# Retuning the issue order of an attention and MLP kernel for a first load as traced and dummy products up to the first k^T v

## The chip, the cores and the metric

The kernel runs on one core of a Trainium2 chip. The metric is the device time of the whole program in microseconds (us), from repeated executions on the chip. "Before" is the kernel without the change and "after" the kernel with it. The engines are called PE (TensorE), PEld (TensorE's weight loads), ACT (ScalarE), DVE (VectorE), POOL (GpSimd) and SP (SyncE). A number such as L870 is a line of the kernel. The change adds eight lines high up, so L870 of before is L878 of after.

## The reference

Eight batches, eight heads, 576 rows (four tiles of 128 and a "tail" of 64), 64 columns per head. Linear attention without a softmax is followed by a normalisation and a residual MLP with a token mixing step.

```python
kv  = einsum('bhsd,bhse->bhde', k, v)                  # k^T v, per head 64 x 64
out = einsum('bhsd,bhde->bhse', q, kv)
x   = out / sqrt(mean(out*out, -1) + 1e-6) * g_norm    # then (b, 576, 512)
a1  = alpha1 * x + beta1
tok = einsum('ts,bsd->btd', w_tok, a1)                 # w_tok: 576 x 576
u   = x + lam * tok
ch  = maximum((alpha2 * u + beta2) @ w_ch1, 0) @ w_ch2 # 512 -> 2048 -> 512
y   = u + lam * ch
```

## The kernel before

The kernel is written as a pool of operations with priorities. When it is built, a small model inside the kernel plays all engines against each other, picks for each free engine the ready operation with the best priority, and so makes one list per engine. On the chip each engine works through its list in order. Semaphores make it wait where an operand is not there yet, and it doesn't look past the operation that waits. So the model's clock, its load times and the priorities decide the order, and the chip decides the time.

The parts that the change touches:

```python
        self.cold = 12.0          # until then a TensorE product is modelled at twice its cost
...
        clock = [3.4]             # when the first load begins to flow
...
        def pe_cost(o):
            if t < self.cold:
                return 2 * o.cost["PE"]
...
            # TensorE has nothing to do now: put a dummy product into its list
            if self.warm is not None and free["PE"] <= t + 1e-9 and t > 0.5:
                o = self.dummy(t, owner)
                if o is not None:
                    seq.append(o)
                    free["PE"] = o.start + (0.43 if t < self.cold else 0.217)
...
def group(o):
    return "%s %s %.2f" % (o.tag, "".join(e[0] for e in sorted(o.cost)), min(o.cost.values()))
ORDER = {                         # corrections to the priority of such a group
    'ch1.0 AD 0.62': 58.4,
    ...
    'wt P 0.03': -1.5,
    'x.01 DP 0.43': -6.1,
}
```

(The comments are mine; three dots are cuts.) The dummy products are there to keep TensorE's clock up while it has nothing to do. They become fixed members of TensorE's list.

The second load, of batch 1, has a modelled time of its own, which the change leaves alone. ScalarE (or VectorE) rounds the loaded q for TensorE:

```python
        def load_q(b, pri, halves=(None,)):
                ...
                    w=STK(i) if x is None else [("st", i, x)], dma_us=3.0 if x is None else 1.5,
                    pri=pri, kind="L")
...
        def round_q(b, pri, halves=((0, 8),)):
                        ...
                        s = st[:, i].rearrange("p (h c d) -> p c h d", h=NH, c=4)
                        return copy_to(e, m, qr[:, c:c + 2, h0:h1], s[:, c:c + 2, h0:h1])
                    ...
                    P.op({"DVE": dve_us(ne, 2), "ACT": act_us(ne)}, f, r=[("st", i, y) for y in hs],
                         w=[("qr", x, y) for x in (c, c + 1) for y in hs], pri=pri, port=True)
...
        round_in(1, -195)         # batch 1: its priority is far ahead of its need
```

Names used below. "Batch 1 k^T v" is L698 before and L706 after. "tok.00" and "tok.01" are the token mixing products of batch 0's two column halves (L998, L1006). "ub" is u in bf16, cast on ScalarE (L494, L502) and transposed on TensorE (L1126, L1134). "The first ch1 product" is the first of `a2 @ w_ch1` (L1167, L1175); from there on TensorE does little but MLP products.

## Time and profile before

| | before |
|---|---|
| time, median of 3 (range) | 352.69 us (352.56 to 352.96) |
| TensorE busy, of a span of 351.1 us | 344.6 us (98%) |
| TensorE's granted clock, 0 to 11 us, 11 to 16 us, after | 0.90, 0.53, 1.00 |
| first k^T v of batch 0 | 11.03 us |
| transposes of w_tok begin | 24.93 us |
| tok.00, batch 1 k^T v begin | 30.65, 34.19 us |
| first ch1 product | 40.78 us |
| from there to the end | 310.3 us |

The table is to be read as two parts, the first 41 us and the 310 us after them. The start of the first ch1 product tells how much an issue order wins or loses in the first part. The prediction below shows the lines.

### The profile page before, as it was taken

The numbers are of one execution on the slowest core, as the hardware profiler recorded it, in microseconds if no ns is written. First come the engines' busy times: TensorE is split into PE (matmuls) and PEld (weight loads), VectorE is DVE, ScalarE is ACT, GpSimd is POOL, SyncE is SP. The second block draws the span as 40 slices with busy tenths as digits, with TensorE's granted clock in tenths as the row PEclk, the third lists the DMA queues.
The fourth block names the chain that finished last, engine by engine and source line by source line (L and its number), as shares of the span: only waits on it lengthen the run. The fifth ranks groups of instructions, "written<-read, shape, count | busy, mean of one in ns | idle before, by whom it ended". The sixth has DMA issues, their size and how long they took to land.

```text
span 351.1 us, 5353 instructions
## 1 busy us (share of the span) xinstructions
PE 344.6 (98%) x2086; PEld 209.3 (60%) x2114; DVE 234.1 (67%) x408; ACT 144.0 (41%) x259; POOL 148.9 (42%) x145
## 2 busy tenths in 40 slices
PE   8899999999999999999999999999999999999996
PEld 3688864567765545647764545547764544457644
DVE  7457589865898786868867778868856683710043
ACT  2653774116823275226722275117731264016500
POOL 3877545027367493147332583148512562140000
PEclk9699999999999999999999999999999999999999
DMA  6899999979935899449952199329922210410022
GB/s 172 255 208 306 206 206 324 186 142 282 226 90 89 206 277 152 93 125 316 200 60 61 74 307 266 65 85 282 264 55 60 83 40 6 100 60 30 2 60 90
DMA packets 90949, 53.62 MB, mean 153 GB/s; under 512 B 56864, under 2 KB 86376, under 8 KB 90924
## 3 DMA queue, kind: packets, MB, share of 16 engines
q1 hardware_dynamic: 60176, 30.81, 36.9%
q0 software_dynamic: 30496, 22.29, 33.4%
q8 instruction: 16, 0.26, 0.3%
q10 hardware_dynamic: 252, 0.18, 0.2%
q14 instruction: 9, 0.07, 0.1%
HBM read 38.20 MB, written 9.44 MB: 136 GB/s over the span
## 4 chain that ended last, share of the span: by engine, by line
PE 96%; DMA 2%; SPq 1%; issue 0%; DVE 0%; ACT 0%
PE ps L1167 36%; PE ps L1195 36%; PE ps L1060 9%; PE ps L689 4%; PE ps L698 2%; DMA st<-in_v_dram 2%; PE ps L998 2%; PE ps L1295 1%; PE ps L1073 1%; PE ps L870 1%; PE ps L898 1%; PE ps L1352 1%; PE ps L967 1%; PE ps L703 1%; PE ps L945 1%
## 5 line engine op out<-in xcount | busy, mean ns | idle before, releaser
L1195 PE MATMUL ps<-w,ht 128*128 128x512 bf16 (+2 forms) x576 | 134.9, 376 | 0.8 <-issue 0.3
L1167 PE MATMUL ps<-a2t,w 128*128 128x320 bf16 (+1 forms) x760 | 133.8, 327 | 0.3
L1167 PEld LDWEIGHTS ps<-a2t,w 128*128 128x128 bf16 x768 | 73.4, 98 | 44.8 <-DVE ht L1153 0.3
L1152 ACT ACTIVATE ht<-ps 128x640 bf16<-128x640 f32 (+1 forms) x106 | 69.0, 653 | 56.6 <-PE ps L1167 55.5
L1195 PEld LDWEIGHTS ps<-w,ht 128*128 128x128 bf16 x592 | 55.9, 98 | 59.6 <-issue 0.8
L1213 POOL TENSOR_TENSOR xm<-xm,lc 128x512 f32<-128x512 f32 x28 | 36.6, 1308 | 95.0 <-DVE lc L1203 94.6
L820 POOL TENSOR_TENSOR xm<-yn,g_bc 128x512 f32<-128x512 f32 x28 | 39.5, 1411 | 47.9 <-DVE yn L815 44.8
L1203 DVE TENSOR_TENSOR lc<-ps,lam_bc 128x512 f32<-128x512 f32 (+2 forms) x37 | 25.0, 675 | 48.8 <-PE ps L1195 44.4
L802 ACT ACTIVATE sq<-ps 128x512 f32<-128x512 f32 (+1 forms) x35 | 20.7, 593 | 36.2 <-PE ps L689 35.9
L689 PE MATMUL ps<-kvc,qt 128*128 128x128 f32 x112 | 32.5, 381 | 0.0
L1065 DVE TENSOR_TENSOR xm<-ps,xm 128x512 f32<-128x512 f32 x28 | 19.0, 689 | 18.3 <-PE ps L1060 17.9
L1060 PE MATMUL ps<-rt,wt 128*128 128x512 bf16 x109 | 30.4, 383 | 0.1
L698 PE MATMUL ps<-vr,kr 128*128 128x128 f32 x112 | 30.3, 386 | 0.0
L804 DVE TENSOR_REDUCE small<-sq 128x8 f32<-128x512 f32 (+1 forms) x35 | 23.6, 676 | 8.4 <-ACT sq L802 8.2
L817 DVE TENSOR_TENSOR rt<-yn,ge 128x512 bf16<-128x512 f32 x27 | 24.4, 912 | 0.4
L815 DVE TENSOR_TENSOR yn<-ps,small 128x512 f32<-128x512 f32 (+1 forms) x35 | 23.9, 689 | 0.8
L689 PEld LDWEIGHTS ps<-kvc,qt 128*128 128x128 f32 x112 | 22.1, 199 | 2.3
L1153 DVE TENSOR_SCALAR ht<-ps 128x512 bf16<-128x512 f32 (+1 forms) x22 | 16.1, 736 | 10.3 <-PE ps L1167 10.2
L698 PEld LDWEIGHTS ps<-vr,kr 128*128 128x128 f32 x112 | 21.6, 200 | 0.8 <-DMA vr<-in_v_dram 0.3
L494 ACT ACTIVATE ub<-xm 128x512 bf16<-128x512 f32 (+1 forms) x17 | 9.3, 563 | 22.5 <-DVE xm L1065 22.4
L1060 PEld LDWEIGHTS ps<-rt,wt 128*128 128x128 bf16 x112 | 10.9, 97 | 11.7
L681 DVE TENSOR_TENSOR st<-st 128x1024 bf16<-128x1024 f32 x12 | 16.2, 1367 | 0.2 <-ACT st L494 0.2
(152 smaller groups left out, 366.1 us busy)
## 6 DMA issues: line engine op xcount, KB each, us to landing
out_dram<-xm SPq DMA_DIRECT2D x31, 256.0 KB, 2.6
kr<-in_k_dram POOLq DMA_DIRECT2D x7, 1024.0 KB, 8.9
vr<-in_v_dram POOLq DMA_DIRECT2D x7, 1024.0 KB, 12.6
st<-in_q_dram SPq DMA_DIRECT2D x7, 1024.0 KB, 9.5
w<-in_moe_w_ch_dram POOLq DMA_DIRECT2D x8, 512.0 KB, 17.5
st<-in_k_dram SPq DMA_DIRECT2D x2, 512.0 KB, 7.2
st<-in_v_dram SPq DMA_DIRECT2D x2, 512.0 KB, 7.7
st<-in_q_dram SPq DMA_DIRECT2D x2, 512.0 KB, 8.7
```

Source lines behind the costliest of these rows:

```text
L689: P.op(F, lambda e, _: e.matmul(t.flat()[:, 128 * pr:128 * pr + 128], a(), m(), start=True, stop=True), r=r, w=[t], kind="F", **kw)
L698: P.op(cost, lambda e, _, h=h, c=c: e.matmul(t.flat()[:, 128 * (h - h0):128 * (h - h0) + 128], flat(kr[:, s, h, c:c + 2, :]), flat(vr[:, s ...
L804: P.op({"DVE": dve_us(512)}, lambda e, _: e.tensor_reduce(out=small[rows, s4], in_=sq[rows, s2], axis=AX.X, op=ALU.add), r=[("sq", s2)], w ...
L815: P.op({"DVE": dve_us(512)}, lambda e, _: e.tensor_tensor(out=hview(yn[rows, s3, :]), in0=hview(t.flat(rows)), in1=bc, op=ALU.mult), r=[t, ...
L817: P.op({"DVE": dve_us(512), "POOL": pool_us(512)}, lambda e, _: e.tensor_tensor(out=rto, in0=yn[rows, s3, :], in1=ge1[rows, :], op=ALU.mul ...
L820: P.op({"POOL": pool_us(512)}, lambda e, _: e.tensor_tensor(out=hview(x), in0=hview(yn[rows, s3, :]), in1=g_bc[rows, None, :].to_broadcast ...
L1060: P.op({"PE": 0.216}, lambda e, _, sc=sc: e.matmul(t.flat(), wt[:, sc, 128 * c:128 * c + 128], rt[:, sc, :] if sc < 4 else rtt[:], start=( ...
L1152: return e.activation(dst, src(), ACT.Relu)
L1167: return e.matmul(o, w1[:, dj, 128 * fj:128 * fj + 128], m, start=(dj == 0), stop=(dj == 3))
L1195: P.op({"PE": 0.004 + n * 0.212 / 512}, lambda e, _: e.matmul(t.flat()[:, 0:n], ht[:, fj, 128 * c:128 * c + 128], w2[:, fj, lo:hi], start= ...
L1203: o = P.op({"DVE": dve_us(n)}, lambda e, _: e.tensor_tensor(out=lc[:, lo:hi], in0=t.flat()[:, 0:n], in1=lam_bc[:, lo:hi], op=ALU.mult), r= ...
L1213: lambda e, _: e.tensor_tensor(out=x, in0=x, in1=lc[:, lo:hi], op=ALU.add),
```

## The change

No operation of the kernel is added or removed. Its own model is corrected with numbers from a trace: the first loads, and the time from which TensorE runs at full clock (5.4 us instead of 12.0). The model now asks for dummies at half their former modelled length between 5.4 and 12 us, so more of them, up to the first k^T v. A new set of priorities was then tuned on that model. The intent is a first stretch in which the model's times are the chip's.

```diff
-        self.cold = 12.0
+        self.cold = 5.4
@@
-        clock = [3.4]
+        clock = [2.6]
@@ ORDER = {
-    'sums.01 P 0.11': 52.5,
-    'tok.01 P 0.12': -17.8,
-    'w1.3 P 0.93': -5.8,
-    'wt P 0.03': -1.5,
+    'qtr.01 AD 0.40': -90.0,
+    'sums.00 A 0.30': -85.1,
+    'sums.01 P 0.11': 37.6,
+    'w2.3 P 0.93': 49.5,
+    'wt P 0.03': -48.7,
     ...                       (21 entries before, 29 after; six keys are in both)
@@ def load(b, pri):             first load, b == 0
-                        w=[f + "ft"], dma_us=1.0, pri=pri, kind="L")
+                        w=[f + "ft"], dma_us=0.8, pri=pri, kind="L")
-                            w=["qft"], dma_us=1.0, pri=pri, kind="L")
+                            w=["qft"], dma_us=0.9, pri=pri, kind="L")
-                        w=[("st", i, x)], dma_us=1.5, pri=pri, kind="L")
+                        w=[("st", i, x)], dma_us=1.9 if x == 0 and f != "v" else 1.35, pri=pri, kind="L")
```

More of the change, by code (lines that the diff above doesn't have):

```diff
@@ L453 @@
 ORDER = {
-    'ch1.0 AD 0.62': 58.4,
-    'ch2.1 S 0.45': -1.4,
-    'norm.1 D 0.69': 53.4,
-    'norm.1 P 0.07': 22.6,
-    'norm.2 D 0.69': -31.4,
-    'norm.5 D 0.69': -65.9,
-    'norm.5 P 1.33': -5.6,
-    'norm.6 DP 0.69': 56.8,
-    'norm.6 P 1.33': 57.3,
-    'qtr.1 P 0.07': -5.1,
-    'qtr.4 DP 0.69': -34.3,
-    'round_in.4 DP 1.23': -28.1,
-    'round_in.5 DP 1.23': -37.9,
-    'sums.01 P 0.11': 52.5,
-    'tok.01 P 0.12': -17.8,
-    'tok.4 D 0.69': 35.8,
-    'tok.5 P 0.22': -10.7,
-    'w1.0 P 0.93': 6.2,
-    'w1.3 P 0.93': -5.8,
-    'wt P 0.03': -1.5,
-    'x.01 DP 0.43': -6.1,
+    'ch1.0 AD 0.62': 60.6,
+    'ch2.3 D 0.69': 8.9,
+    'load.0 DP 0.15': 92.7,
+    'load.0 DP 0.25': 21.1,
+    'load.0 P 0.50': 71.9,
+    'load.1 P 0.93': -6.5,
+    'norm.1 DP 0.69': 64.1,
+    'norm.2 D 0.20': 39.9,
+    'norm.4 D 0.20': 26.5,
+    'norm.5 DP 0.69': 28.6,
+    'norm.5 P 1.33': 36.3,
+    'qtr.00 P 0.12': -31.1,
+    'qtr.01 AD 0.40': -90.0,
+    'qtr.4 DP 0.69': -34.3,
+    'qtr.4 S 2.40': -19.4,
+    'round.01 ADP 0.43': -10.0,
+    'round.t AD 0.45': -55.9,
+    'round_in.3 DP 1.23': 5.0,
+    'sums.00 A 0.30': -85.1,
+    'sums.01 P 0.11': 37.6,
+    'tok.1 P 0.22': 10.9,
+    'tok.5 P 0.22': -29.1,
+    'tok.5 P 0.75': 2.0,
+    'w2.3 P 0.93': 49.5,
+    'wt P 0.03': -48.7,
+    'x.00 D 0.69': -17.1,
+    'x.00 DP 0.69': -3.1,
+    'x.01 D 0.69': 13.5,
+    'x.01 P 1.33': 48.4,
 }
```

## The prediction

> **What bounds the kernel now.** I began with the page of the kernel before: the busy row of the engines, the slices, then the chain of work that ended last.
>
> ```profile
> PE 344.6 (98%) x2086; PEld 209.3 (60%) x2114; DVE 234.1 (67%) x408; ACT 144.0 (41%) x259; POOL 148.9 (42%) x145
> ...
> PEclk9699999999999999999999999999999999999999
> ...
> PE 96%; DMA 2%; SPq 1%; issue 0%; DVE 0%; ACT 0%
> ```
>
> TensorE is busy for 98% of the span and is 96% of the chain. The kernel therefore ends when TensorE has done its real work once at full clock, plus whatever TensorE wasted on the way. The waste is of three kinds: idle, half clock, and dummy products (which count as busy). The clock row shows the second slice alone, 8.8 to 17.6 us, below full. To size the waste I asked for stretches of the span; the columns are the stretch, its length, busy time and count of PE, PEld, DVE, ACT and POOL, granted clock, DMA share and GB/s.
>
> ```profile
> 0.00:11.00 11.00, 8.56 (x22) 2.84 (x22) 7.55 (x20) 3.85 (x7) 4.88 (x17) 0.90 0.71 204
> 11.00:16.00 5.00, 4.97 (x20) 4.44 (x20) 1.74 (x4) 2.96 (x7) 3.75 (x5) 0.53 0.96 289
> 16.00:25.00 9.00, 9.00 (x66) 7.50 (x66) 5.06 (x14) 5.27 (x13) 6.48 (x9) 1.00 0.87 155
> 25.00:41.00 16.00, 15.86 (x147) 13.17 (x148) 11.60 (x28) 7.19 (x14) 10.23 (x15) 1.00 1.36 274
> 41.00:60.00 19.00, 18.95 (x114) 11.79 (x115) 15.26 (x29) 12.90 (x26) 8.68 (x10) 1.00 1.35 258
> ...
> 320.00:351.00 31.00, 28.13 (x175) 16.82 (x174) 7.23 (x12) 7.74 (x11) 0.00 (x0) 1.00 0.13 43
> ```
>
> From 41 us on TensorE idles some 3.8 us of 310, and 2.9 of that is the last stretch, the final multiply, add and store. There is nothing for an issue order to win there beyond about 0.9 us. All else is in the first 41 us. The same stretches asked for the dummy product's line alone give 13 dummies in 16 to 25 us, 8 in 25 to 41 and 1 just after 11; none follows. The timeline of TensorE shows the start:
>
> ```profile
> 1.04 5.35 PE L1295 MATMUL ps<-hot 128*128 128x512 bf16 x14 [1.04 <-DVE hot L1262]
> 6.32 1.98 PE L1308 MATMUL ps<-xm,w 1*128 1x512 f32 x4
> 8.33 0.22 PE L1337 MATMUL ps<-ident,w 8*128 8x8 f32 x1
> 8.49 1.15 PE L1295 MATMUL ps<-hot 128*128 128x512 bf16 x3
> 11.03 0.80 PE L870 MATMUL ps<-vr,kr 128*128 128x256 f32 x2 [1.39 <-ACT vr L494]
> ```
>
> Line 870 is the first k^T v. It waits for the first half of v, which landed at 10.33 us (issued at 2.88, 7.45 under way in the chain), and for a rounding on ScalarE. The dummies stop at 9.64, so TensorE stands idle 1.39 us. Fine stretches place the clock: full at 8.8, half from about 8.85 to about 15.68.
>
> **What the Trainium skill says.** "TensorE: Matmul & The Clock Gate", section "What's actually happening": the array runs at half clock by default, and a free-running window of about 3.4 us with enough activity releases it. The trace agrees: dummies start 0.43 us apart from 1.04 to 5.28 us and 0.22 apart after (the granted clock reads 1.00 throughout, so the spacing is the better witness). 15.68 minus 8.85 is 6.83 us, two such windows. Section "Wait — 56ns, not 53.3ns?" gives 426.7 and 215.7 ns per 512-column product, as here. One thing is not explained by that page: the clock fell at 8.85, before the idle of 1.39 us began, after a window that was nearly all "busy", but 2 us of it with line 1308, fp32 products with one row of the array in use. I suspect that these count for little. "DMA: Bandwidth & Descriptors", section "Issuing engines are not separate DMA queues", says that the queues share the same 16 engines; the trace agrees, with DMA share above 1.3 from 25 to 60 us.
>
> **The change part by part.** No operation of the kernel is added or removed; the kernel holds a small model by which it lists its own instructions when built, and the edit changes that model. (1) The time until which a product costs double goes from 12.0 to 5.4 us. Dummies fill the modelled gaps, so their number follows from it. Before, they were laid at 0.43 us up to the first product: 17, plus two doubled 0.9 us for line 1308. Now, some 10 at 0.43, then (10.0 - 5.4 - 1.8)/0.217, about 13, so 23: 10 x 0.427 + 13 x 0.217 + 1.98 = 9.1 us from 1.04, ending near 10.3 instead of with a 1.39 us gap. The gap shrinks to about half a microsecond. (2) The first loads get the times traced: 2.6 + 0.8 + 2.0 = 5.4 for the first tail against 5.3 traced. The order of these loads does not change, so the first half of v still lands near 10.3 and the first k^T v still starts near 10.9. (3) A new list of priorities. The read-outs of the second half's q^T and the sums of the first half go forward; the transposes of w_tok go forward by 47; the sums of the second half by 15. Weights are fetched in their order of use: of the w1 quarters, 0, 3, 1, 2 becomes 0, 1, 2, 3, and quarter 3 of w2 goes last.
>
> The ledger of what can be won, from 11.03 to the first ch1 product (line 1167) at 40.78 us:
> - Half clock: 4.65 us of products to 15.68, less a dummy of 0.43, is 4.2 us that takes 2.1 at full clock: 2.1 us.
> - Dummies: 21 x 0.216 = 4.5 us, and the slow one 0.4.
> - Idle: 0.2 us.
> Together 7.2 us, which would be 2.0% of the time, if all went and the later 0.9 us stayed.
>
> But not all can go. The w_tok loads wait for the first k's second half, which lands just before 15.84; the last of w_tok lands at 17.35 + 6.3 = 23.7 us by its issue and longest landing, and nothing in the change moves that. Up to then TensorE has only the first batch's attention. At full clock, by the durations in the trace: 20 k^T v x 0.117 = 2.3; 20 q transposes, 2.1; sums, 8 products and 20 small ones, 3.3; 20 outputs x 0.11 = 2.2; about 9.9 us. So 12.7 - 9.9 = 2.8 us stay idle or dummy whatever the order. What is left is at most 7.2 - 2.8 = 4.4 us, with 0.9 more later on.
>
> How much of it comes? At full clock the first half is through about 2 us sooner, and the second half's sums and outputs (13 small sums and 10 outputs, 2.5 us, that ran at 26.9 to 30.6, behind the transposes of w_tok) can now be done under the w_tok load. That is the main gain: what was done after w_tok goes into dummy time before it. I put it at 2 us. The 1.7 us of dummies between 31 and 40 us sit in waits on VectorE's additions (line 1008) and casts, with the chain w_tok, transposes, copy, row sums, w_tok's last row, tok, add, cast, transpose, which does not get shorter; I count 0.7. Line 1352 started at 24.93 where w_tok was there at 23.7, worth up to 1 us, of which I count 0.4. Sum: 3.1 us, so 352.7 - 3.1 = 349.6 us. First ch1 product then near 38.
>
> **The rivals.** (A) The clock falls all the same. If line 1308 counts for little, the window up to 8.85 is as empty as before: before it held about 1.3 us of dummies, and 1.4 would be there now. The next window is full, so the clock would be back at 12.26 rather than 15.68. Half the clock's gain goes, and late dummies at 0.43 us would even delay the first k^T v by up to 0.7 us. For it: the fall came before the idle. Against: only one window, and its phase is free. Time: 350.5 to 351.5, since the w_tok landing hides part of the loss. (B) The weights become the bound. Quarter 0 of w1 lands at 25.7 + 12.3 = 38.0 us (the shortest landing of its line); ch1 at 40.78 has 2.8 us to spare, a ch1 at 38 none. The loads run at a DMA share above 1.3, so they do not come sooner. Against: k^T v and q transposes of batch 1 (some 4.5 us) land at 34 to 35 us and can fill in. It caps the gain near 3 us rather than reversing it. (C) The list fits the model and not the chip: the start gains, but displaced read-outs make TensorE stall after 41 us, where it now loses 0.9 us in 270. Time: 351 to 353. (D) Everything works, 4.4 us and some of the 0.9: 347.5.
>
> **Range and chances.** The rivals A, B and C all lie above my figure and D below. I take 347.4 to 351.9. Being over 2% faster means under 345.6, 7.1 us, which is about the whole ledger; the w_tok landing forbids most of it: 4%. Over 2% slower would need a new stall of 7 us in a kernel that keeps all its work: 1%.
>
> **What would show it.** Right: about 23 dummies before the first k^T v, which starts within 0.4 us of 10.9; granted clock 1.00 from 11 to 16 us; fewer than 14 dummies after it, against 22; the transposes of w_tok (line 1352 there) starting near 23.8 with most sums of the second half ahead of them; first ch1 product at 37.5 to 39; idle after 41 us still near 3.8 us. Wrong: clock 0.5 up to 12.3 (A); TensorE waiting on a DMA of w before ch1 (B); more than 1.5 us of idle between 41 and 320 us (C); or the first k^T v clearly earlier than 10.6, which would mean that the loads themselves had moved.

## The result, and the profile after

| | before | after |
|---|---|---|
| time, median of 4 (range) | 352.66 us (352.56 to 352.96) | 356.37 us (355.01 to 357.50) |
| span of the profiled run | 351.1 us | 355.7 us |
| first k^T v of batch 0 | 11.03 us | 12.71 us |
| transposes of w_tok begin | 24.93 us | 24.36 us |
| tok.00 begins | 30.65 us | 30.24 us |
| batch 1 k^T v begins | 34.19 us | 38.56 us |
| first ch1 product | 40.78 us | 44.69 us |
| from there to the end | 310.3 us | 311.0 us |

The ratio of after to before is 1.0102 (95% interval 1.0064 to 1.0140). A ratio here and below is the mean time of one kernel's runs over the mean of the other's runs of the same rounds, so it is not quite the ratio of the medians that I quote. Executions over 1.5% slower than the fastest of the same kernel are left out of the means. The kernel after is 3.7 us slower, within 2%, and outside the predicted range.

The page of after, with the same rows as shown of before (busy, granted clock in 40 slices, chain of work that ended last):

```profile
PE 349.1 (98%) x2126; PEld 209.4 (59%) x2126; DVE 236.3 (66%) x408; ACT 145.0 (41%) x261; POOL 148.0 (42%) x143
...
PEclk9899899999999999999999999999999999999999
...
PE 87%; DMA 7%; DVE 2%; POOL 1%; SPq 1%; ACT 1%; issue 0%
```

TensorE's share of the chain fell from 96% to 87%, and DMA's rose from 2% to 7%. Some load now stands in the path. The clock row has two dips, in slices 2 and 5, where before had one. Slice 5 is 35.6 to 44.5 us. The same stretches as before, up to 60 us (columns: the stretch, its length, busy time and count of PE, PEld, DVE, ACT and POOL, granted clock, DMA share, GB/s):

```profile
0.00:11.00 11.00, 9.94 (x25) 3.20 (x26) 7.62 (x19) 3.83 (x6) 3.76 (x17) 0.89 0.74 201
11.00:16.00 5.00, 5.00 (x30) 3.38 (x28) 2.66 (x8) 1.55 (x4) 4.76 (x4) 0.89 0.92 300
16.00:25.00 9.00, 9.00 (x71) 7.76 (x70) 6.82 (x16) 5.40 (x14) 7.03 (x10) 1.00 0.89 157
25.00:41.00 16.00, 13.60 (x104) 10.34 (x103) 7.90 (x18) 6.01 (x12) 11.61 (x16) 0.89 1.38 274
41.00:60.00 19.00, 19.00 (x137) 13.29 (x136) 13.94 (x29) 12.78 (x28) 4.99 (x5) 1.00 1.28 259
```

The fourth line holds the loss: from 25 to 41 us TensorE is idle 16.00 - 13.60 = 2.40 us, where it was idle 0.14, and its clock is 0.89 instead of 1.00. The stretches that the change aimed at, the first two, did not come out as aimed either (0.89 from 11 to 16 us, not 1.00), but the third is full.

The timeline of TensorE at the start (start, length, engine, line, operation; in brackets the idle time ahead of it and what ended it). The dummies are L1303, the one-row fp32 products L1316, the first k^T v L878:

```profile
8.23 1.92 PE L1303 MATMUL ps<-hot 128*128 128x512 bf16 x5
10.09 0.27 PE L1345 MATMUL ps<-ident,w 8*128 8x8 f32 x1
10.29 2.77 PE L1303 MATMUL ps<-hot 128*128 128x512 bf16 x8
12.71 0.47 PE L878 MATMUL ps<-vr,kr 128*128 128x256 f32 x1
```

The eight dummies ahead of the first k^T v run at half clock. Fine stretches of the trace put the clock at half from 8.67 to 12.08 us, one window of 3.41 us, and again from 35.97 to 39.39. The first k^T v comes 1.7 us later than before, but those dummies are only part of the reason. In before, ScalarE rounds all of the first half of v. In after, VectorE rounds a part of it, behind a memset that waits for a small load and behind five more operations (before's ScalarE, then after's VectorE, with the operations between left out):

```profile
10.35 1.15 ACT L494 ACTIVATE vr<-st 128x512 fp32r<-128x512 f32 x2 [0.38 <-DMA st<-in_v_dram]
```

```profile
8.26 0.91 DVE L1279 MEMSET yn<- 64x1024 f32 x1 [1.93 <-DMA yn<-in_moe_beta_dram]
...
11.17 0.84 DVE L503 CAST vr<-st 128x512 fp32r<-128x512 f32 x1
```

This v landed at 9.81 us, and VectorE is done with it at 12.01. So about 1.0 of the 1.7 us would be there without any dummy, and about 0.7 is the dummies. Three runs below with the same list up to this point and full clock in it agree: in the profiles of s_act, a_q0 and q_right the first k^T v comes at 11.85, 11.77 and 12.53 us, after waits of 0.63, 0.58 and 1.39 us for this rounding.

Yet tok.00, whose first product came at 30.65 us in before, starts at 30.24, and its last ends at 33.57 instead of 34.19. The kernel after is 0.6 us **ahead** at 33.6 us. The next lines of TensorE's timeline:

```profile
33.19 0.38 PE L1006 MATMUL ps<-rtt,wt 128*128 128x256 bf16 x2
35.98 0.37 PE L1134 MATMUL ps<-identb,ub 128*128 128x128 bf16 x2 [2.40 <-ACT ub L502]
36.15 1.06 PE L1303 MATMUL ps<-hot 128*128 128x512 bf16 x2
```

TensorE waits 2.40 us for ScalarE's cast of ub, and then transposes it between dummies at half clock. ScalarE in after, over the same time:

```profile
29.76 0.28 ACT L960 ACTIVATE rs<-ps,eps 128x20 f32<-128x20 f32 x1
34.47 1.06 ACT L502 ACTIVATE qr<-st 128x1024 fp32r<-128x1024 f32 x1 [4.43 <-DMA st<-in_q_dram]
35.44 0.40 ACT L502 ACTIVATE ub<-xm 128x256 bf16<-128x256 f32 x1
```

The cast of ub stands behind the rounding of batch 1's q, and that waits 4.43 us for q to land. The load was issued at 21.88 us and took 12.6 us. The operand of the cast itself was ready long before: VectorE's first addition there (L1016) ran from 31.81 to 32.22 us. So the cast is 3.2 us late for no reason of its own.

Now the same time in the kernel before, first ScalarE, then TensorE:

```profile
34.57 2.00 ACT L494 ACTIVATE qr<-st 128x1024 fp32r<-128x1024 f32 x2 [4.12 <-DMA st<-in_q_dram]
36.48 1.32 ACT L494 ACTIVATE ub<-xm 128x256 bf16<-128x256 f32 x4
```

```profile
33.81 0.38 PE L998 MATMUL ps<-rtt,wt 128*128 128x256 bf16 x2
34.19 0.44 PE L698 MATMUL ps<-vr,kr 128*128 128x128 f32 x2
...
38.37 0.39 PE L1126 MATMUL ps<-identb,ub 128*128 128x128 bf16 x4
```

ScalarE waits as long there (4.12 us) and casts ub even later, at 36.48. But TensorE's list has the batch 1 k^T v and tok.01 next, 34.19 to 38.37 us, and only then the transposes of ub. The wait was there, and nobody saw it. After has the two in the other order: transposes and six dummies first, then k^T v and tok.01.

The whole loss can be added up on TensorE: 0.62 us ahead at the end of tok.00, then 2.40 idle, then 2.58 for the transposes and dummies at half clock (35.98 to 38.56), then 6.13 to the first ch1 product (38.56 to 44.69) where before took 6.59 from the same point (34.19 to 40.78). That is -0.62 + 2.40 + 2.58 - 0.46 = 3.90, and 44.69 - 40.78 = 3.91. The rest of the 4.6 us between the two profiled spans, 0.7, lies after it.

### The profile page after: what moved, and what is told of

It reads as the page before. It is cut to its first block, busy times and chain, and to the rows that moved or that the text cites. A ratio compares the mean times of both kernels' runs of the same rounds, so it can differ in the third digit from the quotient of the medians.

```text
span 355.7 us, 5389 instructions
## 1 busy us (share of the span) xinstructions
PE 349.1 (98%) x2126; PEld 209.4 (59%) x2126; DVE 236.3 (66%) x408; ACT 145.0 (41%) x261; POOL 148.0 (42%) x143
## 4 chain that ended last, share of the span: by engine, by line
PE 87%; DMA 7%; DVE 2%; POOL 1%; SPq 1%; ACT 1%; issue 0%
PE ps L1203 36%; PE ps L1175 33%; PE ps L1068 9%; DMA st<-in_q_dram 6%; PE ps L697 3%; PE ps L706 2%; DMA a2t<-in_moe_w_tok_dram 1%; PE ps L1081 1%; DVE rt L825 1%; PE ps L1303 1%; PE ps L1006 1%; ACT qr L502 0%; PE ps L711 0%; DVE ht L1161 0%; SPq L637 0%; DVE small L812 0%
## 5 line engine op out<-in xcount | busy, mean ns | idle before, releaser
L1203 PE MATMUL ps<-w,ht 128*128 128x512 bf16 (+2 forms) x592 | 137.4, 376 | 0.0
L1221 POOL TENSOR_TENSOR xm<-xm,lc 128x512 f32<-128x512 f32 x28 | 38.0, 1356 | 94.5 <-DVE lc L1211 94.3
L828 POOL TENSOR_TENSOR xm<-yn,g_bc 128x512 f32<-128x512 f32 x28 | 40.9, 1459 | 46.4 <-DVE yn L823 45.5
L1068 PE MATMUL ps<-rt,wt 128*128 128x512 bf16 x112 | 31.9, 385 | 0.0
L706 PE MATMUL ps<-vr,kr 128*128 128x128 f32 x112 | 31.1, 392 | 0.0
L825 DVE TENSOR_TENSOR rt<-yn,ge 128x512 bf16<-128x512 f32 x25 | 22.7, 916 | 0.5
L706 PEld LDWEIGHTS ps<-vr,kr 128*128 128x128 f32 x112 | 22.4, 205 | 0.9 <-issue 0.3
L502 ACT ACTIVATE ub<-xm 128x512 bf16<-128x512 f32 (+1 forms) x22 | 11.9, 560 | 20.0 <-DVE xm L1073 19.5
L1303 PE MATMUL ps<-hot 128*128 128x512 bf16 x50 | 18.3, 497 | 1.1 <-DVE hot L1270 1.1
L771 DVE TENSOR_TENSOR qt<-st 128x512 fp32r<-128x512 bf16 x22 | 17.4, 829 | 0.1
```

The source lines that it names most:

```text
L706: P.op(cost, lambda e, _, h=h, c=c: e.matmul(t.flat()[:, 128 * (h - h0):128 * (h - h0) + 128], flat(kr[:, s, h, c:c + 2, :]), flat(vr[:, s ...
L825: P.op({"DVE": dve_us(512), "POOL": pool_us(512)}, lambda e, _: e.tensor_tensor(out=rto, in0=yn[rows, s3, :], in1=ge1[rows, :], op=ALU.mul ...
L828: P.op({"POOL": pool_us(512)}, lambda e, _: e.tensor_tensor(out=hview(x), in0=hview(yn[rows, s3, :]), in1=g_bc[rows, None, :].to_broadcast ...
L1068: P.op({"PE": 0.216}, lambda e, _, sc=sc: e.matmul(t.flat(), wt[:, sc, 128 * c:128 * c + 128], rt[:, sc, :] if sc < 4 else rtt[:], start=( ...
L1203: P.op({"PE": 0.004 + n * 0.212 / 512}, lambda e, _: e.matmul(t.flat()[:, 0:n], ht[:, fj, 128 * c:128 * c + 128], w2[:, fj, lo:hi], start= ...
L1221: lambda e, _: e.tensor_tensor(out=x, in0=x, in1=lc[:, lo:hi], op=ALU.add),
```

## The experiments

**Theory 1**: the loss is the second load. Batch 1's q lands later than the model thinks (after's model, run again from its source, lets it land at 28.05 us; in the trace of after it lands at 34.45), ScalarE's list stalls on it with the ub casts behind it, and TensorE's new list has nothing ahead of the ub transposes to do meanwhile. **Theory 2**: the loss is the clock, which fell although the change counts on it; late dummies delayed the start. **Theory 3**: the new list is bad over the whole kernel, not in this place. The runs were made in five groups. The kernel before had medians of 352.66, 353.30, 353.97, 352.75 and 353.36 us in them, over 7 to 12 runs each. The number of 3.41 us windows at half clock differs from run to run, in before too: a mean granted clock of 0.995 is one window, 0.990 two, 0.981 four, and before took 352.4 to 353.6 us at 0.995 and 356.1 to 356.9 at 0.981 in the last two groups (one more, at 0.990, took 357.1). This sets the width of the intervals.

In the edits below, `shift(ops, last)` puts operations right behind another in the finished lists, everything else unchanged.

**s_act: ScalarE's two q roundings behind the ub casts.**

```diff
+    shift([o for o in seq if o.tag == "round_in.1" and o.eng == "ACT"],
+          [o for o in seq if o.tag == "tok.00" and o.eng == "ACT"][-1])
```

> The changed kernel, with one thing moved: ScalarE's two roundings of batch 1's q are issued behind the last of its casts of the first half's rows (ub) instead of before and between them; every other engine keeps its list. Theory 1 (the loss is a list made for a q load that the model lets land at 28 us and that lands at 34.5 us: ScalarE waits for it with the casts behind it, and TensorE's list has the transposes of these rows ahead of batch 1's k^T v and of the second half's tok): the 2.4 us of TensorE idle near 34 to 36 us go, the clock does not fall at 36 us, the first ch1 product comes at 41 to 41.7 us instead of 44.7, and the time is 352.5 to 353.6 us. Theory 2 (the late first k^T v, 12.7 instead of 11.0 us, behind dummies at half clock, is what costs): no change, 355.0 to 357.5 us.

Measured: 353.83 us (353.71 to 355.92), ratio 1.0031 (1.0004 to 1.0059). About 2.5 of the 3.7 us come back, some 1.2 do not. Theory 1 has the direction and most of the size, but less than it expected. The wait at 34 us is gone in the profile, which is no proof by itself: it is the slowest of the five runs, with the clock at half from 27.60 to 34.42 us, so that tok.00 ended at 36.23 us, when q was there, and the first ch1 product came at 43.34 and not at 41 to 41.7.

**s_pe: TensorE's first ub transposes and dummies behind the batch 1 k^T v.** The other half of the same stall: ScalarE still waits for q, but TensorE has something to do.

```diff
+    early = [ut.0 transposes and dummies that stand ahead of the 7th tok.01 product]
+    shift(early and the copies that read them, behind the 6th tok.01 product)
```

> The changed kernel, with TensorE's list alone changed: the first eight transposes of the ub rows and the six dummies among them are issued behind 14 of batch 1's k^T v and 6 tok products of the second half, roughly where the kernel before has them; ScalarE still waits for the q load. Theory 1: TensorE now waits only for batch 1's v, which lands at 34.8 us, so some 1.3 us idle instead of 2.4 and no fall of the clock at 36 us; first ch1 product at 41.3 to 42.5 us; time 352.8 to 354.2 us. Theory 2: no change, 355.0 to 357.5 us.

Measured: 355.35 us (354.71 to 355.71), ratio 1.0071 (1.0045 to 1.0097). The idle time at 34 us fell to 0.74 us, but 0.58 was added at the next place (a tok.01 product that waits for VectorE's copy of a transpose), and the first ch1 product came at 42.05 us in a profile of 352.9 us. A partial repair, and a miss of its expected range.

**s_drop: after without the last eight dummies before the first k^T v.**

```diff
+    late = [dummies ahead of the first kv.00 product][-8:]
+    P.sequence = [o for o in P.sequence if o not in late]
```

> The changed kernel without the last eight dummies ahead of the first k^T v. Theory 1: the first k^T v comes at 10.6 to 11.2 us instead of 12.7, but the w_tok load at 16 us waits for the same k landing, so the first transposes of w_tok stay within 0.6 us of 24.4 and the time within 0.8 us of 356.4. Theory 2: the time falls by 1.5 us or more, to 354.9 or less.

Measured: 357.23 us (356.20 to 357.87), ratio 1.0123 (1.0094 to 1.0152). The first k^T v came at 12.36, not at 10.6 to 11.2 us, since it then waits 1.64 us for VectorE's rounding of v. The clock was at half from 8.05 to 18.29 us, three windows, and w_tok's transposes began 2.2 us later than in after. Even so the first ch1 product came at 43.41 us, 1.3 **earlier** than in after. The edit hardly made the start earlier, so it is a weak test of Theory 2. s_row (next), which has after's lists from the first k^T v on, says more: there tok.00 ended at 38.12 us, 4.5 us later than in after, and the first ch1 product came at 45.23, only 0.5 us later. Between the two lie 7.11 us, without a wait, where after takes 11.12. A late start disappears in the wait for q. A late start as the cause of the loss, Theory 2, finds no support.

**s_row: after with the one-row fp32 products behind the dummies.** This asks what made the clock fall at 8.67 us.

```diff
+    rows = [load.0 products of TensorE ahead of the first kv.00 product]
+    shift(rows and their copies, behind the last dummy ahead of kv.00)
```

> The changed kernel with the three small fp32 products of the start (two that spread a row, with one row of the array in use, and a small transpose) moved behind all the dummies that precede the first k^T v, with their read-outs. Clock theory (a window filled by these products is taken as idle): with 26 dummies in a row, the clock does not fall near 8.7 us; it stays full to about 12.1 us and falls there, since the window from 8.7 to 12.1 us holds the 2.2 us of one-row products, to come back at about 15.5 us. Rival (the fall near 8.7 us has another cause, such as a fixed time after the start): it falls near 8.7 us as before. Time, whichever holds: within 1 us of 356.4, since the loss later remains.

Measured: 356.81 us (354.99 to 357.81), ratio 1.0108 (1.0067 to 1.0150), so no gain. The stretches (TensorE alone: length, busy, granted clock, DMA share, GB/s) answer the question:

```profile
5.00:9.00 4.00, 4.00 (x18) 1.00 0.97 297
9.00:12.50 3.50, 2.29 (x7) 1.00 1.14 290
12.50:16.00 3.50, 3.50 (x14) 0.51 0.91 304
```

The one-row products now stand at 9.06 to 11.04 us. The clock stays full until 12.55 us, the end of the window that holds them and 1.2 us of idle time, and then falls for one window. In before the window that ended at 8.85 was busy for 3.37 of 3.41 us, 1.98 of it with the one-row products and 1.31 with dummies; in after that of 8.67 was busy throughout, 2.24 with one-row products. A window that holds hardly anything but dummies (5.73 to 9.14 here) is not followed by a fall. So the fall moved with the one-row products. It does not always follow them. In the first window at full clock of the 20 profiles, the clock fell at the end of the 15 in which dummies fill at most 1.5 us (after 1.45, before 1.31), and held after the five in which they fill 1.7 us or more (new_list 1.7 beside 1.75 of one-row products; s_act, a_q0 and q_right, with after's list up to here, 1.7 to 1.8). So in these windows it is the dummies that count, and the one-row products seem to count for little more than idle time. Where a window's edges fall in the list differs from run to run, and with it whether the clock falls: that part is luck.

**q_right: after with the model told the real landing of batch 1's q.**

```diff
-                    w=STK(i) if x is None else [("st", i, x)], dma_us=3.0 if x is None else 1.5,
+                    w=STK(i) if x is None else [("st", i, x)], dma_us=(5.0 if b == 1 else 3.0) if x is None else 1.5,
```

> The changed kernel with one number of its own model more: batch 1's q load is given 5.0 us of transfer instead of 3.0, so that the model lets it land at 34.05 us and batch 1's v at 34.05 us, as traced (34.5 and 34.8). The new lists then have ScalarE cast all five ub rows ahead of both q roundings, and TensorE has batch 1's k^T v behind the second half's tok. Theory 1 (the list was made for loads that come too soon): no idle above 1.5 us between 30 and 41 us, no fall of the clock after 16 us that starts in an idle stretch, first ch1 product at 39.2 to 40.8 us, time 350.8 to 352.8 us. Rival 3 (the new model and list are bad elsewhere too, the late loads are only one of several faults): 353.5 us or more.

Measured: 358.76 us (357.85 to 359.34), ratio 1.0128 (1.0060 to 1.0195). The stall at 34 us is gone, and in the profiled run the clock never fell, but the list that the model makes now has new waits between 160 and 200 us, 2.6 us of idle there, most of it this (line of the waits of TensorE, 150 to 210 us: total, times, longest):

```profile
PE ps L1175 <- DVE ht L1161: 2.0, 2, 1.8
```

One number in the model reshuffles the list to the end of the kernel. The priorities were tuned for the other number. My expectation was wrong, and the run is no test of Theory 1; it shows that Theory 3's mechanism exists.

**old_list, new_list, old_list_q: model and priorities exchanged.** The first has before's priorities with after's model, the second after's priorities with before's model, the third is before with batch 1's q at 5.0.

> The kernel before with both model edits (5.4 us, first loads as traced) and its own old list of priorities. TensorE's list then has batch 1's k^T v and the second half's tok ahead of the transposes of ub, as in the kernel before, though ScalarE still has both q roundings ahead of the casts. Theory 1: nothing of weight waits for the casts, so the time is that of the kernel before within 0.8 us, 352.0 to 353.5 us. Theory 2 (the model edits, with their dummies at half clock, are the fault): 355 us or more.

> The kernel before with its own model and the new list of priorities. ScalarE then has both q roundings ahead of seven ub casts, TensorE has nearly all of the second half's tok ahead of most transposes and batch 1's k^T v behind them, among ch1. Theory 1: the casts again wait for the q load (34.5 us) and its roundings (to 36.5), with nothing left for TensorE but dummies, so it idles some 2 us between 34 and 38 us; 353.5 to 356 us, and the lower end if the clock holds. Theory 2: as before, 352 to 353 us, since the model is the old one.

> The kernel before, old model and old list, with only batch 1's q load given 5.0 us, which makes the model let it land at 35.0 us. Theory 1: the lists now fit the landing, but the priorities were found for another list, and batch 1's k^T v comes behind the transposes; no idle for the q load near 34 to 36 us; time 351.8 to 353.8 us. Rival: if a right q landing alone were worth the whole difference, it would be below the kernel before by 1 us or more.

Measured: old_list 356.94 us, but two of its four runs fell in the slow state and the fast two are 352.55 and 356.02, ratio 1.0003 (0.9903 to 1.0103): inconclusive. new_list 357.07 us (354.54 to 358.27), ratio 1.0072 (1.0002 to 1.0142), with 1.22 us of the same wait for ub between 33 and 41 us. The new priorities thus bring the stall with either model of the first load. What it costs here is less clear: the interval just leaves 1, two of the four runs are at 0.981, and the profiled run has its first ch1 product at 40.89 us, as before. old_list_q 354.01 us, ratio 0.9995 (0.9941 to 1.0050): as before.

**a_q0: the wait taken away, the lists untouched.** s_act moved two instructions. Here every engine keeps after's list, but the two q roundings of batch 1 read batch 0's q, which landed long ago (the result is wrong).

```diff
-                        s = st[:, i].rearrange("p (h c d) -> p c h d", h=NH, c=4)
+                        s = st[:, 0 if b == 1 else i].rearrange("p (h c d) -> p c h d", h=NH, c=4)
     # and, in the finished lists, these two operations no longer depend on the load of q
```

> After with every engine's list untouched, but ScalarE's two q roundings of batch 1 read the first batch's q, which has long landed, and wait for no load (the result is wrong on purpose). Theory 1 (q that lands late stalls the in-order list): the 2.4 us wait of TensorE at 34 us is gone, first chunk product at 41 to 42.3 us, time 352.9 to 354.0 at one clock fall, ratio 1.000 to 1.004. Rival (the list is bad whatever lands when): 355.5 to 357, first chunk product beyond 43.5.

Measured: 354.52 us (354.35 to 355.09), ratio 1.0052 (1.0040 to 1.0064). ScalarE's timeline has the rounding at 31.02 us, without a wait, and the cast when VectorE has added:

```profile
31.02 1.05 ACT L502 ACTIVATE qr<-st 128x1024 fp32r<-128x1024 f32 x1
33.85 0.42 ACT L502 ACTIVATE ub<-xm 128x256 bf16<-128x256 f32 x1 [1.78 <-DVE xm L1017]
```

TensorE has no wait from 30 to 45 us, and its first ch1 product comes at 42.32. By the times, about half of the loss (1.02% to 0.52%) goes when only the wait for q goes, with no change of order; the two intervals just touch. Some of this is the clock: all five runs have a clock of 0.994 or 0.995, one window, and of after's four only one has (355.01 us). Of the 1.5 us that stay at the first ch1 product, 1.0 is there at the end of tok.00 already (35.20 us against 34.19), since in this run the one half-clock window lay under the w_tok work (27.80 to 31.22 us). The other 0.5 comes between there and the first ch1 product, where the dummies among the ub transposes (1.0 and 0.6 us at 35.15 and 36.13 us) stand ahead of the batch 1 k^T v. With tok.00 that late, after's own wait would have been shorter too, so the profile does not give the worth of the landing; the times do.

**s_lean and s_fix: after with two and with three repairs.** s_lean is s_act without the dummies behind the first tok.00 product. s_fix also has the transposes behind the batch 1 k^T v, as s_pe.

```diff
+    shift(...)                                   # as s_act
+    gone = [dummies behind the first tok.00 product of TensorE]
+    P.sequence = [o for o in seq if o not in gone]
     # s_fix: and shift(...) as s_pe
```

> After, with ScalarE's two q roundings behind the last ub copy (as in s_act) and without the dummy products that stand in TensorE's list behind the first product of token half 0. Theory 1 (late q load and list order; dummies that fall in a half-clock stretch cost 0.43 us each of path): first chunk product at 40.6 to 42.0 us, time 352.4 to 353.6 where one clock fall is met. Rival (what was left of the loss after s_act has nothing to do with the head): 353.7 to 354.2, as s_act.

> After with three repairs: ScalarE's q roundings behind the last ub copy, TensorE's first ub transposes behind the k^T v of batch 1, and no dummies behind the first product of token half 0. Theory 1 (the whole loss lies in the list between 33 and 45 us): first chunk product at 40.2 to 41.8, time 352.2 to 353.4, ratio 0.997 to 1.001. Rival (some 1 us of the loss lies elsewhere): ratio 1.002 to 1.004.

Measured: s_lean 354.13 us (353.19 to 355.49), ratio 1.0010 (0.9966 to 1.0055): the loss is no longer to be seen in the times, within half a per cent (its profile still has the first ch1 product at 42.12 us, 1.3 later than before's). s_fix 355.27 us (352.98 to 357.53), ratio 1.0072 (1.0041 to 1.0103), which misses its expected range. Its profile has two more half-clock windows right there (36.81 to 43.64 us). In both, a wait of TensorE stands where after had its own (s_lean, waits of TensorE from 30 to 45 us):

```profile
PE ps L706 <- DVE xtl L1016: 1.4, 1, 1.4
```

L706 is the batch 1 k^T v. The profile names VectorE, but v of batch 1 lands just there: it was issued at 19.1 us and took 16.0, and the k^T v starts at 35.20. In s_fix it is 19.4 + 15.7 = 35.1 and 35.19. In the kernel before it is 19.0 + 15.2 = 34.2 and 34.19. So whoever comes early to the batch 1 k^T v waits for v.

**s_v27, s_v30, b_v30: the q load issued later, so that v lands earlier.** If q and v share the DMA, v gains when q comes later. In s_v27 and s_v30 (s_lean otherwise) the q load waits for ScalarE's copies of w_tok or for its square root, and was issued at 29.65 and 30.63 us instead of 21.54. b_v30 is the same in the kernel before, with b_lean's edit (below).

```diff
+    ld = [o for o in seq if o.tag == "load.1" and o.eng == "SP"]
+    gate = [o for o in seq if o.tag == "wt" and o.eng == "ACT"][-1]    # s_v30, b_v30: "sums.01"
+    ld[0].deps.add(gate); shift(ld[:1], gate)
+    shift(ACT's round_in.1, behind ACT's first ut.0 copy)
```

> s_lean (after, q roundings moved, late dummies gone) with the q load of batch 1 issued only after ScalarE's last copy of the w_tok transposes, at about 27.4 us instead of 21.5, and its roundings behind the first a2t copy. If the landing of v is the floor: v lands 1 to 1.5 us earlier, the 1.4 us wait ahead of the k^T v of batch 1 shrinks under 0.5, first chunk product near 41, 0.7 to 1.4 us less than s_lean (352.2 to 353.0). Rival (v lands no earlier, or another wait takes its place): within 0.4 us of s_lean, wait still over 1.

> As s_v27, with the q load behind ScalarE's square root at about 30 us. If v is the floor: v lands 1.5 to 2 us earlier, no wait ahead of the k^T v of batch 1; but q lands at 38 to 39 us, and if that is too late TensorE waits for its transposes after 42 us, 0 to 1 us. Time 352.0 to 353.5.

> b_lean with the q load behind ScalarE's square root. The kernel before reaches its k^T v of batch 1 at 34.2 to 34.5 us, just as v lands, so an earlier landing alone frees nothing: within 0.5 us of b_lean (ratio to before 0.995 to 1.000). If it is over 0.7 us faster than before in these runs, it is the version that beats both.

Measured: 361.15 us (360.46 to 363.22), 362.21 and 360.16 us, ratios 1.0213, 1.0240 and 1.0191 (intervals from 1.013 to 1.030). I had not foreseen this. v did land early (in s_v27 18.9 + 11.3 = 30.2 us, 11.3 us under way instead of 16.0; this shows the sharing, which a DMA share above 1.3 alone, as in the prediction, does not), and the batch 1 k^T v began at 34.1 instead of 35.2 us. But q landed at 43.28 us, and the stall of after came back in a larger size, now for the ub of tok.01 (s_v27: ScalarE's timeline, then the waits of TensorE from 28 to 50 us):

```profile
43.28 2.00 ACT L502 ACTIVATE qr<-st 128x1024 fp32r<-128x1024 f32 x2 [6.86 <-DMA st<-in_q_dram]
```

```profile
PE ps L1134 <- ACT ub L502: 6.7, 1, 6.7
PE ps L706 <- DVE xm L1016: 0.5, 1, 0.5
```

As a test of the floor these runs say little: with v there at 30.2 us, the k^T v came only 1.1 us sooner, because it then waited for VectorE's additions. As a test of Theory 1 they say more than planned. The same line, ub of ScalarE behind a rounding that waits for q, costs TensorE nothing with q moved out of the way (a_q0), 2.40 us with q at 34.5 (after) and 6.7 us with q at 43.3, and it makes the kernel **before** 6.8 us slower too (b_v30, the same 6.7 us wait on its L1126).

**b_lean, b_nodum: the same repairs in the kernel before.** b_nodum takes the 7 dummies behind the first tok.00 product away, b_lean moves ScalarE's roundings behind the ub casts as well.

> The kernel before, with ScalarE's two q roundings behind the first ub copies and without the dummy products behind the first product of token half 0 (7 of them, all at full or half clock between 34 and 41 us). Theory 1: the dummies were on TensorE's path there, 0.21 to 0.43 us each, less what ub or v would have made it wait: 0.3 to 1.0 us less than before. Rival (the dummies only filled waits): within 0.3 us of before.

> The kernel before without the 7 dummies behind the first product of token half 0, nothing moved. If the dummies were b_lean's gain: ratio 0.995 to 0.999, 0.4 to 1.5 us less than before. If ScalarE's moved roundings were it: within 0.3 us of before.

Measured: b_lean 352.78 us (352.09 to 353.25) where before had 353.97, ratio 0.9967 (0.9935 to 1.0000). b_nodum 352.68 us (351.90 to 356.23) where before had 352.75, ratio 1.0008 (0.9974 to 1.0043). b_lean has the lowest ratio of all kernels run and beats after; that it beats before is likely and not shown, for its interval touches 1 and two of the eleven runs of before were at the lowest clock. b_nodum's interval holds both of its expectations, so what made b_lean's gain is not decided.

**b_warm, b_both: the change's intent with the old list.** Before's lists, with 13 more dummies ahead of the first k^T v and one of the two one-row products moved away. b_both adds b_lean's edit.

```diff
+    for n in range(13):                          # 16 dummies there instead of 3
+        P.sequence.insert(behind the last dummy ahead of kv.00, one more dummy)
+    shift(the lam product and its copy, behind the last kv.01 product)
```

> The kernel before's lists with 13 more dummy products ahead of the first k^T v (16 instead of 3 in that place) and one of the two one-row fp32 products moved behind the second k^T v: the change's intent alone, with the old list behind it. If full clock up to and through the first k^T v shortens the path: 1.5 to 2.1 us less than before. If the w_tok landing gates what follows: first k^T v near 11.0 us at full clock, but w_tok transposes begin where they did (24 to 25 us), gain under 0.7 us. If the clock falls anyway: no gain, up to 1.5 us slower.

> b_lean and b_warm together. Sum of the two gains: 0.3 to 1.7 us less than before (351.0 to 352.4 on a chip where before takes 352.7). Rival: nothing adds up, because the w_tok and q landings set the head's end; then as b_lean.

Measured: b_warm 355.56 us (354.30 to 356.53), ratio 1.0047 (1.0010 to 1.0084); b_both 354.27 us, ratio 1.0015 (0.9976 to 1.0054). The timeline of b_warm:

```profile
8.53 0.22 PE L1337 MATMUL ps<-ident,w 8*128 8x8 f32 x1 [0.95 <-DMA w<-in_moe_beta_dram]
8.68 5.31 PE L1295 MATMUL ps<-hot 128*128 128x512 bf16 x16
13.64 0.59 PE L870 MATMUL ps<-vr,kr 128*128 128x256 f32 x2
```

The clock fell at 9.13 us all the same, after a window with 2.46 us of products, 1.12 of them one-row, and the extra dummies ran at half clock. The first k^T v came 2.6 us late. The transposes of w_tok then came 2.8 us late (27.69 against 24.93) and the first ch1 product 3.0 us (43.75 against 40.78). A second fall, at 26.19 us, follows the window in which the moved one-row product now stands (22.72 to 23.84; in b_both a fall at 25.18 follows it), so the edit is not the dummies alone. The change's intent, tried in this form with the old list, cost the kernel 0.5%.

## Why the prediction was wrong

The prediction was 349.6 us with a range up to 351.9; the time is 356.37.

**The ledger of before held.** Everything to be won lies ahead of the first ch1 product: the remainder after it stayed at 310.3 to 311.6 us in before, after and the eleven other profiles in which that product still marks the end of the head (s_act, s_pe, s_drop, s_row, s_lean, s_fix, a_q0, b_lean, b_warm, b_both, b_nodum). The spans follow its start.

**Step 1, the dummies and the clock, failed as rival A described, and for a second reason.** The prediction put 23 dummies before the first k^T v and the clock at full from 11 to 16 us. There were 26, the clock fell at 8.67 and was back at 12.08 (the rival said 12.26), and the first k^T v came at 12.71 instead of 10.9. The rival's 0.7 us for late dummies is about what they cost (12.01 to 12.71). The other 1.0 us nobody foresaw: "the first half of v still lands near 10.3 and the first k^T v still starts near 10.9" took the rounding of v for granted, and the new list put a part of it behind VectorE's wait for a small load. s_row supports the suspicion about L1308 behind the rival; that a run meets this fall is a matter of where the windows lie.

**"I put it at 2 us", the second half's sums and outputs under the w_tok load, did not happen.** In after all ten small sums and all ten outputs of the second half come behind the first transposes of w_tok (26.78 to 30.24 us); in before it was nine and ten (not 13 and ten, as the prediction counts).

```profile
24.36 0.67 PE L1360 MATMUL ps<-identb,a2t 128*128 128x128 bf16 x9
...
26.78 0.94 PE L953 MATMUL ps<-sel,vr 128*128 128x4 f32 x7
```

From the first transpose of w_tok to tok.00 after takes 5.88 us and before 5.72. Dummies behind the first k^T v were to be fewer than 14 and are 24 (21 in before, which the ledger counts as 21 and a slow one). What after made up it made up earlier: 11.65 us from the first k^T v to the transposes of w_tok, where before takes 13.90. With 14 dummies in either, these 2.25 us are about the 2.1 us that the ledger counts for before's half clock there; after had its own half clock ahead of the first k^T v. So at 33.6 us it was 0.6 us ahead, 2.5 us short of the 3.1; that it was ahead at all is not the main gain come true.

**The step that failed outright is the one about the second load.** The prediction says of batch 1's k^T v and q transposes that they "land at 34 to 35 us and can fill in", and counts a landing at 34 to 35 us as a help. It asked what TensorE could do with them, and not who would stand still until they came; and its chain "tok, add, cast, transpose, which does not get shorter" has the cast follow the addition, where in after it came 3.2 us later. The new list put ScalarE's rounding of that q ahead of the ub casts and the ub transposes ahead of the batch 1 k^T v. TensorE idled 2.40 us, the clock fell for it, and dummies at half clock followed. With the wait for q taken out (a_q0) 1.9 of the 3.7 us go, with ScalarE's order changed (s_act) 2.5, and with the late dummies gone as well (s_lean) the loss cannot be told from zero. With q later still (s_v27, b_v30) the same wait grows to 6.7 us, in either kernel.

**Rival C had the mechanism and the wrong place.** "The list fits the model and not the chip" is what happened. Rival C looked for the stall after 41 us and capped the loss at 353. It lay at 33.6 to 39.4 us, in the stretch that I had already booked as gain. After's idle between 41 and 320 us is 0.25 us, less than before's 0.9.

**Could the gain have been had?** Only partly, by these runs. In before the batch 1 k^T v starts at the landing of v (34.19 us), so an earlier end of tok.00 has to be filled with other work. s_lean shows the waiting that results (1.4 us) and s_v27 that VectorE's additions are the next thing, only 1.1 us ahead of it. No variant of either list got to its ch1 products for good before 40.45 us (b_lean; in b_v30 a first one ran at 38.86, ahead of the 6.7 us stall). The 38 us of the prediction were not in reach of any order that was tried.

**What stays open.** The part of the loss that a_q0 leaves, 0.5%, is split for its profiled run alone (1.0 us with the half-clock window under the w_tok work, 0.5 behind tok.00), not for the times: s_pe and s_fix, which repair the order further, came out worse than s_lean, and s_fix met two half-clock windows in the place in question. Why the clock falls after a window filled with w_tok transposes and small sums in one run and not in the next is not settled either.

## What to carry to other kernels

When engines work through fixed lists, a model that is corrected for one load only makes a list that trusts its wrong time for the next load: check, for every load in the stretch that is retuned, the modelled landing against the traced one, and ask which instructions stand behind the first reader on that reader's engine. A wait that costs nothing today, such as ScalarE's 4.12 us for q in the kernel before, is a trap for the next order; look for the long waits of the engines that are not the bottleneck before moving anything around them. Dummy products in a fixed list are not free filler: they run at half speed when the clock falls, as the eight ahead of after's first k^T v did. And a model that is given the traced loads still has to place the engine that reads them: look at what that engine waits for just before.

## What the Trainium skill lacked or had wrong

- "TensorE: Matmul & The Clock Gate", "What's actually happening", ties the clock to windows that are busy or idle. It doesn't say how little one-row products count. In after the window of 5.26 to 8.67 us was busy for all of its 3.41 us, 2.24 of it with one-row fp32 products, and the clock fell; moved to 9.06 us (s_row), they took the fall along to 12.55. Nor does it say how much of a window must be busy: in the first window at full clock of these profiles, up to 1.5 us of dummies in 3.41 went with a fall and 1.7 us or more with none. The free-running 3.41 us window itself agrees with the traces: the clock fell at whole windows from its first record in each.
- The same page, "Why this matters for your kernels", warns of idle gaps over about 3 us. In after a gap of 2.40 us, in a window busy for 1.02 of its 3.41 us, was enough for a fall (35.97 us).
- The same page, "Part 4: PE-mode transpose", says that transposes don't count as busy in the usual way. The traces neither confirm nor refute it: the window ahead of the fall of s_act at 27.60 us was nearly full, 2.02 us with transposes of w_tok and 1.10 with four-column sums, and so was that of a_q0 at 27.80 (2.43 and 1.05), but q_right had such a window too, up to 27.72 us (2.48 and 0.92), and its clock held. No run here tells the two kinds of product apart.
- The same page, "Architectural detail: the array is 16× 32×32, not 1× 128×128", states that ScalarE's queue is strictly first in, first out. The traces agree (a cast ready at 32.22 us ran at 35.44 behind a rounding that waited for q). No page says what that costs when a cast stands behind a rounding: here TensorE waited 2.40 us, and 6.7 us with q later (s_v27).
- No page says what the granted clock reads before its first record in a trace: the first record of before is at 5.43 us, and `prof` takes 1.00 for the time ahead of it, where before's dummies start 0.43 us apart, the half-clock spacing.
